# Six of the loads' input arrays laid out in DRAM as eight groups of sixteen rows

## Chip, core and metric

The kernel runs on one core of a Trainium2 chip. The metric is device time in microseconds of one execution. A difference of 2% is about 10 us here.

## What is computed

Two batches, 12 heads, 448 tokens, head width 64. First an attention whose scores are mixed across heads before the softmax and whose weights are mixed across heads after it; its output, as rows of 768 channels, goes through a mixer block and a gated block. Everything is float32; some weights arrive as float64 and are turned into pairs of rounded parts on the chip.

```
scores = scale * q @ k^T;  scores = einsum('bhij,hg->bgij', scores, w_pre)
attn = softmax(scores);    attn = einsum('bhij,hg->bgij', attn, w_post);  x = attn @ v
u = x + token mixing (relu(x^T w_tok1) w_tok2)^T;  x = u + relu(u w_ch1) w_ch2
h = gelu(x w_in); u, v = halves of h; v = layernorm(v) * g
out = x + (u * (w_sg v + b_sg)) w_out
```

## The kernel before

The order of all work is written out by hand; each engine runs its instructions in that order and waits on semaphores. The attention fills about the first 200 us and the three later blocks the rest.

**Chunks.** The queries of a batch are cut into four chunks of 120, 120, 120 and 88 (`CH`), so there are eight chunks. For one chunk, `qk` (matmuls of line 328) makes the scores of two heads at a time and a copy (line 333) puts them into a tile S, with 128 query slots on the partitions and 12 heads by 448 keys along each row.

**Steps.** To mix across heads, heads have to lie on partitions. So a chunk is cut into steps of 20 queries, 46 steps in all. For each step `b_dma` (line 360) issues two transfers, SBUF to SBUF, from S into a tile P of a ring of six: each reads ten partitions of S and writes 120 partitions of P, 12 heads for each query. `b_pre` (line 368) multiplies P by the mixing weights, the vector engine takes the row maximum (373), the scalar engine exponentiates (381), GpSimd makes the normalising weights (388 to 394), `b_post` (line 415) multiplies by the second mixing and transposes back in 64 small matmuls, and a copy (425) puts the result into AT. When a chunk's steps are done, `av` (lines 450 and 459) multiplies AT by v.

**The loop.** At index i the loop issues, if they are due, one `qk` of the next chunk, `b_pre` of step i+2, `b_post` of step i and then the transfers of step i+5 (`LD` = 5, `LP` = 2). A tile of the P ring is free again three steps later, so the P transfers can be three steps ahead of their matmul and no further. All DMAs but one are issued by SyncE (SP) in program order: the P transfers and the loads of q, k, v and weights share that queue.

**The loads.** q of one chunk comes in two loads (`load_q`, line 308), k of one batch in six (`load_k`, 315), v of one batch in three (`load_v`, 304). The list `loads` says at which index i each is issued: index -4 and -3 the third chunk's q, 1 and 3 the first batch's second and third v, 4 to 6 the fourth and fifth chunks' q and the first token weight (`w_dma`, line 99), 9 to 14 the second batch's k, and so on to 29. Four pieces of token weights (`w_tok1`, `w_tok2`) are loaded during the attention. The first three pieces of the channel weights are loaded by

```
        if 0 < i + LD - NB <= RB:
            w_dma()
```

with NB = 46 and RB = 3, thus at i = 42, 43 and 44. Every one of these loads writes 128 partitions from a DRAM array whose first axis has 128 rows.

**Layouts on the host.** `layouts` transposes the inputs before the launch; the arrays that it returns are the kernel's DRAM tensors.

Of the kernel before, what the change touches and what calls it, by code (L numbers as in the profile page):

```python
# [19 lines left out]
LD, LP = 5, 2  # L20
NP_BUFS = 2 * (LD - LP + 1)

WB, RB, SQ = 3, 3, 5
# [4 lines left out]


@with_exitstack  # L30
def tile_kernel(ctx, tc, q, k, v, w_pre, w_post, w_tok1, w_tok2, w_ch1, w_ch2,
                w_u, w_v, g_ln, w_sg, b_sg, w_out, out):
    nc = tc.nc
    B, D, H, S = 2, 64, 12, 448
    P = 128
# [1 line left out]
    C = H * D  # L37
    NCC = C // P
    T = B * S
    TOK = w_tok1.shape[2]  # L40
    NF = w_ch1.shape[1]
    DH = w_v.shape[2]
    ND = DH // P
# [2 lines left out]
    CH = [(0, 120), (120, 120), (240, 120), (360, 88)]  # L46
# [167 lines left out]
    def piece(src, pr, a, n, scale=None, dst=None):  # L214
        pieces.append([src, pr, a, n, scale, dst])
        return len(pieces) - 1
# [5 lines left out]
    NS = 4  # L222
    def tok_dst(n, pr, a, w):
        return lambda: [shared[:pr, 2 * n + j, :a * w].rearrange("p (a n) -> p a n", a=a) for j in range(2)]

    p_t1 = [piece(w_tok1[:, i:i + 2], P, 2, TOK, dst=tok_dst(i // 2, P, 2, TOK)) for i in range(0, NS, 2)]
    p_t2 = [piece(w_tok2[:, i:i + 1], P, 1, S, dst=tok_dst(NS // 2 + i, P, 1, S)) for i in range(TOK // P)]
    wvt = {}

    def wv_dst(cc):  # L230
# [68 lines left out]
    QG = 3  # L299
    NQ = NP // QG  # L300

    def load_v(b, g):
        t = vn[b, g] = ap_.tile([P, 14 * D], F32, tag=f"vn{g}", name=f"vn{b}_{g}")
        nc.sync.dma_start(out=t, in_=v[b, :, g])

    def load_q(b, c, g, eng=nc.sync):
        t = qn[b, c, g] = qp.tile([P, QG, P], F32, tag=f"qn{g}", name=f"qn{b}_{c}_{g}", bufs=2)
        eng.dma_start(out=t, in_=q[b, :, c, g * QG:(g + 1) * QG])

    KG = [(i, 1) for i in range(NP)]  # L310

    def load_k(b, g):
        i, n = KG[g]
        x = qp.tile([P, n, S], F32, tag=f"kn{g}", name=f"kn{b}_{g}")
        nc.sync.dma_start(out=x, in_=k[b, :, i:i + n])
        for j in range(n):
            KX[b, i + j] = x[:, j]

    def qk(x, i, pool=psM, copies=(nc.scalar.copy,)):

        b, c = chunks[x]
        if i == 0:
            SS[b, c] = qp.tile([P, SWC], F32, tag="S3", name=f"S{b}_{c}") if x % 3 == 1 else big(f"S{b}_{c}", F32)
        nm = f"qk{b}_{c}_{i}"
        ps = pair(nm, pool)
        for cols in HALVES:
            for j, rows in enumerate(HALVES):
                nc.tensor.matmul(ps[cols, j, :S], lhsT=qn[b, c, i // QG][rows, i % QG, cols], rhs=KX[b, i][rows],  # L328
                                 start=True, stop=True)
        n = 2 // len(copies)  # L330
        for j, copy in enumerate(copies):
            o = (2 * i + j * n) * S
            copy(SS[b, c][:, o:o + n * S].rearrange("p (j s) -> p j s", j=n), ps[:, j * n:(j + 1) * n, :S])  # L333
# [10 lines left out]
    NB = len(steps)  # L344
# [161 lines left out]
    for g in range(NQ):  # L506
        load_q(0, 1, g)
    load_const()
    load_v(0, 0)


# [14 lines left out]
    for x in range(NCH):  # L526
        if x < 2:
            at = [-LD - 1 + x] * NP
            for i in range(NP):
                n = x * NP + i  # L530
# [45 lines left out]
    for i in range(-LD, NB):  # L576
        for fn, a in extra.get(i, []):
            fn(*a)
        ahead = 0 <= i + LP < NB
        due = list(scores.get(i, []))  # L580
        if due:
            qk(*due.pop(0))
        if ahead:
            b_pre(i + LP)
        next_turn(i, 0)
        if ahead:
            b_max(i + LP)
        if 0 <= i + 1 < NB:
            b_norm(i + 1)
        for d in due:  # L590
            qk(*d)
        if i >= 0:
            b_post(i)
        if ahead:
            b_exp(i + LP)
        if i >= 0:
            b_turn(i, nc.scalar.copy if i - END in AT_ACT else nc.vector.tensor_copy)
            next_av(i)
        next_turn(i, 1)
        if i + LD < NB:  # L600
            b_dma(i + LD)
        for fn, a in loads.get(i, []):
            fn(*a)
        if 0 < i + LD - NB <= RB:
            w_dma()
        if i >= 8 and wstate["conv"] <= p_t2[-1]:
            pump(1)
        if i + LD == first[chunks[-1]] - 1:
            XR = [big(f"x{nm}0") for nm in "hl"]
            X[0] = [t[:, :XW] for t in XR]  # L610
            RX[0] = [t[:, XW + 16:XW + 16 + TOK // P * C].rearrange("p (t c) -> p t c", c=C) for t in XR]
        if i + LD == NB:
            qctx.close()
            wctx = ctx.enter_context(ExitStack())
            wpool = wctx.enter_context(tc.tile_pool(name="wp", bufs=1, side="right", reuse_waits="tile"))
            wstate["open"] = True
# [43 lines left out]
    with ExitStack() as mctx:  # L660
        mp = mctx.enter_context(tc.tile_pool(name="tok", bufs=1, reuse_waits="tile"))
        RR = {}
        def tok1(b, turns=()):
# [3 lines left out]
            got, pss = [], []  # L667
            for tt in range(TOK // P):
                ts = slice(tt * P, (tt + 1) * P)
# [12 lines left out]
            rest = [x[:, (NS - 1) * C:XW] for x in (xh, xl)]  # L682
            for tt in range(TOK // P):
                ts = slice(tt * P, (tt + 1) * P)
# [10 lines left out]
        def tok2(b):  # L695
# [3 lines left out]
            for cc in range(NCC):  # L699
                cs = slice(cc * P, (cc + 1) * P)  # L700
                ps = bank(f"t2ps{b}_{cc}")
                mm3(ps[:, :S], [((rh[:, tt, cs], rl[:, tt, cs]), t2[tt]) for tt in range(TOK // P)])
                U[cc, b] = later(add_split(cc, b, ps[:, :S], uh, ul))
# [211 lines left out]
def layouts(q, k, v, w_pre, w_post, moe_w_tok1, moe_w_tok2, moe_w_ch1, moe_w_ch2,  # L915
            moe2_w_in, moe2_g_ln, moe2_w_sg, moe2_b_sg, moe2_w_out):

    import numpy as np

    def bits(a):  # L920

        return a.view(np.uint64) if a.dtype == np.float64 else a

    def rows(a, p):

        return bits(a).reshape(-1, p, a.shape[1]).transpose(1, 0, 2)

    def blocks(a):

        n = a.shape[0] // 128 * 128  # L930
        return rows(np.concatenate([a, a[n:]]), 128)

    def cols(a, p):

        return bits(a).reshape(a.shape[0] // p, p, -1, p).transpose(1, 2, 0, 3)

    def diagonal(w):
        h = w.shape[0]
        t = np.zeros((2, 64, h, 5), w.dtype)
        for i in range(5):  # L940
            t[:, h * i:h * (i + 1), :, i] = w
        return t

    def spread(a):

        n = a.shape[-1]
        full, rest = n // 10, n % 10 // 2
        t = np.zeros((*a.shape[:-1], 128), a.dtype)
        rows = t[..., :120].reshape(*a.shape[:-1], 10, 12)
        rows[..., :full] = a[..., :10 * full].reshape(*a.shape[:-1], 10, full)  # L950
        if rest:
            rows[..., :rest, full:full + 2] = a[..., 10 * full:].reshape(*a.shape[:-1], rest, 2)
        t[..., :120] = rows.reshape(*a.shape[:-1], 120)
        return t

    def tokens(w):

        t = np.concatenate([w.T, w.T])
        return t.reshape(-1, 128, t.shape[1]).transpose(1, 0, 2)

    B, H, S, D = q.shape
    qt = q.reshape(B, H // 2, 2, S, D).transpose(0, 2, 4, 1, 3).reshape(B, 2 * D, H // 2, S)
    qt = np.stack([spread(qt[..., s:s + 120]) for s in range(0, S, 120)], 2)
    whole = S // 128 * 128
    vs = v.reshape(B, H // 4, 2, 2, S, D)
    vt = vs[..., :whole, :].reshape(B, H // 4, 4, S // 128, 128, D).transpose(0, 4, 1, 2, 3, 5)
    vr = v.reshape(B, 2, H // 4, 2, S, D)[..., whole:, :].transpose(0, 1, 4, 2, 3, 5).reshape(B, 128, H // 4, 2 * D)
    vt = np.concatenate([vt.reshape(B, 128, H // 4, -1), vr], -1)
    wp = diagonal(w_pre).transpose(0, 1, 3, 2).reshape(2, 64, 60)
    wp = np.pad(wp, ((0, 0), (0, 0), (0, 4)))  # L970
    wp[0] = np.roll(wp[0], 4, 0)
    wq = diagonal(w_post).reshape(128, 60)
    half = moe2_w_in.shape[1] // 2
    arrays = {
        'q': qt,
        'k': k.reshape(B, H // 2, 2, S, D).transpose(0, 2, 4, 1, 3).reshape(B, 2 * D, H // 2, S),
        'v': vt,
        'w_pre': wp.reshape(128, 64),
        'w_post': wq,
        'w_tok1': blocks(moe_w_tok1),  # L980
        'w_tok2': rows(moe_w_tok2, 128),
        'w_ch1': cols(moe_w_ch1, 128),
        'w_ch2': cols(moe_w_ch2, 128),
        'w_u': cols(np.ascontiguousarray(moe2_w_in[:, :half]), 128),
        'w_v': rows(np.ascontiguousarray(moe2_w_in[:, half:]), 128),
        'g_ln': moe2_g_ln.reshape(-1, 128).T,
        'w_sg': tokens(moe2_w_sg),
        'b_sg': moe2_b_sg.reshape(1, S),
        'w_out': cols(moe2_w_out, 128),
    }  # L990
    return {n: np.ascontiguousarray(a) for n, a in arrays.items()}
# [34 lines left out]
```

## Time and profile before

| | us |
|---|---|
| median of 3 runs | 508.65 |
| lowest and highest | 505.95 and 512.27 |
| the profiled execution's own time | 511.61 |
| its span, first to last instruction | 509.8 |

The span holds 14006 instructions. TensorE (PE) is busy for 95% of it, VectorE for 67%, ScalarE for 46%, GpSimd for 41%. The 16 DMA engines move 63.84 MB. Times below are in us from the span's start; "issue" as a releaser means that the engine waited for nothing that the profile shows, and SPq is SP's queue of DMA instructions.

### The profile page before, as it was taken

How to read it: one execution, taken by the hardware profiler on the slowest of the kernel's cores; microseconds unless marked ns; L12 is line 12 of the kernel's file. 1: busy time of each engine (PE TensorE's matmuls, PEld its weight loads, DVE VectorE, ACT ScalarE, POOL GpSimd, SP SyncE). 2: the span in 40 equal slices, each digit the busy share in tenths (PEclk: the TensorE clock that was granted, in tenths of full speed). 3: DMA queues.
4: the chain of work that ended last, by engine and by line, in shares of the span. 5: the costliest groups of instructions: out<-in, count | busy, mean ns of one | idle time of the engine just before them, and what ended most of it. 6: DMA issues, size and time to landing. Idle time of an engine off the chain costs nothing.

```text
span 509.8 us, 14006 instructions
## 1 busy us (share of the span) xinstructions
PE 485.2 (95%) x6010; PEld 411.8 (81%) x6010; DVE 342.6 (67%) x452; ACT 236.5 (46%) x457; POOL 208.7 (41%) x292
## 2 busy tenths in 40 slices
PE   9987999989799889999999999999999999999997
PEld 5455677756577569999999999999999998888896
DVE  4574566657365645963657687789887964897882
ACT  3675576576466434462434443333332345454320
POOL 2355256365355420284123322444554434258400
PEclk9999999999899999999999999999999999999999
DMA  6788364455523500310234343353432323103122
GB/s 225 231 227 232 139 219 154 153 200 179 171 112 139 205 4 2 125 63 27 98 103 145 125 143 105 123 165 101 149 123 88 119 73 124 32 0 123 68 85 109
DMA packets 26306, 63.84 MB, mean 125 GB/s; under 512 B 2900, under 2 KB 19844, under 8 KB 26244
## 3 DMA queue, kind: packets, MB, share of 16 engines
q1 hardware_dynamic: 26100, 62.75, 37.0%
q8 instruction: 47, 0.77, 0.6%
q10 hardware_dynamic: 144, 0.20, 0.1%
q14 instruction: 15, 0.12, 0.1%
HBM read 40.83 MB, written 2.75 MB: 85 GB/s over the span
## 4 chain that ended last, share of the span: by engine, by line
PE 89%; issue 4%; ACT 2%; DVE 2%; DMA 1%; POOL 1%; SPq 0%; POOLq 0%; ACTq 0%
PE qk L328 8%; PE post L415 8%; PE av L450 6%; PE c1ps L632 6%; PE c2ps L632 6%; PE pre L368 6%; PE c2ps L634 6%; PE c1ps L634 6%; PE c2ps L633 6%; PE c1ps L633 6%; PE ups L633 2%; PE ups L632 2%; PE ups L634 2%; PE vps L634 2%; PE vps L633 2%
## 5 line engine op out<-in xcount | busy, mean ns | idle before, releaser
L156 POOL TENSOR_TENSOR wl<-cv,wh 128x768 fp32r<-128x768 f32 x28 | 52.6, 1878 | 132.0 <-ACT wh L153 100.6
L415 PEld LDWEIGHTS post<-wt,E 60*64 60x64 f32 x2880 | 54.3, 138 | 31.8 <-issue 23.6
L381 ACT ACTIVATE E<-pre,nm 128x448 f32<-128x448 f32 x90 | 56.3, 632 | 37.3 <-DVE nm L373 33.4
L415 PE MATMUL post<-wt,E 60*64 60x60 f32 (+1 forms) x2880 | 56.3, 221 | 10.5 <-issue 8.3
L373 DVE TENSOR_REDUCE nm<-pre 128x2 f32<-128x896 f32 (+1 forms) x46 | 49.1, 1068 | 24.0 <-PE pre L368 22.2
L135 DVE SCALAR_TENSOR_TENSOR cv<-raw,cv 128x768 uint32<-128x768 uint32 (+2 forms) x44 | 53.1, 1207 | 1.2
L328 PE MATMUL qk<-kn,qn 64*64 64x448 f32 x384 | 50.0, 565 | 3.2 <-issue 1.9
L632 PE MATMUL c1ps<-uh,wh 128*128 128x448 f32 x144 | 52.3, 363 | 0.0
L632 PE MATMUL c2ps<-r1h,wh 128*128 128x448 f32 x144 | 52.3, 363 | 0.0
L368 PE MATMUL pre<-P,wp 64*64 64x448 f32 (+1 forms) x360 | 50.7, 547 | 1.7 <-ACT E L381 1.1
L634 PE MATMUL c2ps<-r1h,wl 128*128 128x448 f32 x144 | 52.2, 362 | 0.0
L634 PE MATMUL c1ps<-uh,wl 128*128 128x448 f32 x144 | 52.2, 362 | 0.0
L633 PE MATMUL c1ps<-ul,wh 128*128 128x448 f32 x144 | 51.8, 360 | 0.0
L633 PE MATMUL c2ps<-r1l,wh 128*128 128x448 f32 x144 | 51.8, 360 | 0.0
L425 DVE COPY AT<-post 128x840 f32<-128x840 f32 (+1 forms) x42 | 44.0, 1047 | 9.7 <-PE post L415 9.6
L113 ACT ACTIVATE cv<-raw 128x768 f32<-128x768 f32 (+2 forms) x44 | 36.1, 821 | 26.9 <-POOL wl L156 19.9
L388 POOL TENSOR_SCALAR rc<-sm 128x2 f32<-128x2 f32 (+1 forms) x46 | 10.5, 229 | 90.2 <-ACT E L381 89.7
L333 ACT COPY S<-qk 128x896 f32<-128x896 f32 x42 | 38.0, 905 | 17.4 <-PE qk L328 15.4
L137 DVE SCALAR_TENSOR_TENSOR cv<-raw,cv 128x768 uint32<-128x768 uint32 (+2 forms) x44 | 40.3, 915 | 1.0
L153 ACT CAST wh<-cv 128x768 fp32r<-128x768 f32 x28 | 23.4, 835 | 34.8 <-DVE cv L137 33.9
L655 DVE SCALAR_TENSOR_TENSOR r1l<-c1ps,r1h 128x448 fp32r<-128x448 f32 x24 | 15.0, 624 | 30.6 <-ACT r1h L653 30.6
L450 PE MATMUL av<-AT,vn 128*64 128x120 f32 (+1 forms) x576 | 32.5, 266 | 2.0 <-issue 1.9
(148 smaller groups left out, 1035.3 us busy)
## 6 DMA issues: line engine op xcount, KB each, us to landing
P<-S SPq DMA_DIRECT2D x88, 210.0 KB
raw<-in_w_ch_dram SPq DMA_DIRECT2D x24, 768.0 KB
raw<-in_w_v_dram SPq DMA_DIRECT2D x6, 512.0 KB
raw<-in_w_u_dram SPq DMA_DIRECT2D x4, 768.0 KB
raw<-in_w_out_dram SPq DMA_DIRECT2D x6, 512.0 KB
qn<-in_q_dram SPq DMA_DIRECT2D x15, 192.0 KB
kn<-in_k_dram SPq DMA_DIRECT2D x12, 224.0 KB
vn<-in_v_dram SPq DMA_DIRECT2D x6, 448.0 KB
```

Source lines behind the costliest of these rows:

```text
L135: nc.vector.scalar_tensor_tensor(fi, lo, 29, fi, op0=ALU.logical_shift_right, op1=ALU.bitwise_or)
L156: nc.gpsimd.tensor_tensor(dst[1], f, f32(dst[0]), op=ALU.subtract)
L328: nc.tensor.matmul(ps[cols, j, :S], lhsT=qn[b, c, i // QG][rows, i % QG, cols], rhs=KX[b, i][rows], start=True, stop=True)
L368: nc.tensor.matmul(ps[cols, e, :S], lhsT=wp[rs], rhs=ring[(2 * i + r) % NP_BUFS][rs], start=True, stop=True)
L373: nc.vector.tensor_reduce(out=st[i]["nm"][:, :ne], in_=st[i]["pre"][:, :ne, :S], axis=AX.X, op=ALU.max, negate=True)
L381: nc.scalar.activation(t, st[i]["pre"][:, e, :S], AF.Exp, bias=st[i]["nm"][:, e:e + 1], scale=1.0, accum_out=sm[:, e:e + 1])
L415: nc.tensor.matmul(ps[cols, r, o:o + w.stop - w.start], lhsT=E[rs, t * 64:(t + 1) * 64], rhs=wt[rs, w], start=True, stop=True)
L425: copy(dst, src)
L450: nc.tensor.matmul(into(hp, x, j), lhsT=vn[b, hp // 2][:, ((hp % 2 * 2 + j) * NH + s) * D:][:, :D], rhs=at[:, s * H + 2 * hp + j, :cols], ...
L632: nc.tensor.matmul(ps, lhsT=lh, rhs=rh, start=(start and i == 0), stop=False)
L633: nc.tensor.matmul(ps, lhsT=lh, rhs=rl, start=False, stop=False)
L634: nc.tensor.matmul(ps, lhsT=ll, rhs=rh, start=False, stop=(stop and i == n - 1))
```

## The change

The arrays `q` (from the third chunk on), `k` (second batch), `v` (both), `w_tok1` and `w_tok2` are laid out as 8 groups of 16 rows with one row of zeros behind each group, and the loads read `[:, :16]` of them. The first two chunks of q and the first batch of k become arrays of their own, `q0` and `k0`, with 128 plain rows. The destinations in SBUF and the indices at which the loads are issued are as they were. The condition on `w_dma` becomes `NB - RB <= i`, thus i = 43, 44 and 45.

```diff
-    p_t1 = [piece(w_tok1[:, i:i + 2], P, 2, TOK, dst=tok_dst(i // 2, P, 2, TOK)) for i in range(0, NS, 2)]
-    p_t2 = [piece(w_tok2[:, i:i + 1], P, 1, S, dst=tok_dst(NS // 2 + i, P, 1, S)) for i in range(TOK // P)]
+    p_t1 = [piece(w_tok1[:, :16, i:i + 2], P, 2, TOK, dst=tok_dst(i // 2, P, 2, TOK)) for i in range(0, NS, 2)]
+    p_t2 = [piece(w_tok2[:, :16, i:i + 1], P, 1, S, dst=tok_dst(NS // 2 + i, P, 1, S)) for i in range(TOK // P)]
...
-        nc.sync.dma_start(out=t, in_=v[b, :, g])
+        nc.sync.dma_start(out=t, in_=v[b, :, :16, g])
...
-        eng.dma_start(out=t, in_=q[b, :, c, g * QG:(g + 1) * QG])
+        n = b * len(CH) + c
+        src = q0[:, n] if n < 2 else q[:, :16, n - 2]
+        eng.dma_start(out=t, in_=src[..., g * QG:(g + 1) * QG, :])
...
-        nc.sync.dma_start(out=x, in_=k[b, :, i:i + n])
+        nc.sync.dma_start(out=x, in_=k[:, :16, i:i + n] if b else k0[:, i:i + n])
...
-        if 0 < i + LD - NB <= RB:
+        if NB - RB <= i:
             w_dma()
...
+    def apart(a, d=0):
+
+        a = a.reshape(*a.shape[:d], 8, 16, *a.shape[d + 1:])
+        t = np.zeros((*a.shape[:d + 1], 17, *a.shape[d + 2:]), a.dtype)
+        t[(slice(None),) * (d + 1) + (slice(16),)] = a
+        return t
...
-        'q': qt,
-        'k': k.reshape(B, H // 2, 2, S, D).transpose(0, 2, 4, 1, 3).reshape(B, 2 * D, H // 2, S),
-        'v': vt,
+        'q0': qt[:, :2],
+        'q': apart(qt[:, 2:]),
+        'k0': kt[0],
+        'k': apart(kt[1]),
+        'v': apart(vt, 1),
...
-        'w_tok1': blocks(moe_w_tok1),
-        'w_tok2': rows(moe_w_tok2, 128),
+        'w_tok1': apart(blocks(moe_w_tok1)),
+        'w_tok2': apart(rows(moe_w_tok2, 128)),
```

## Rows read from the trace of the kernel before

**Rows 1.** The page, busy time and share of the span of TensorE.

```profile
PE 485.2 (95%) x6010; PEld 411.8 (81%) x6010; DVE 342.6 (67%) x452; ACT 236.5 (46%) x457; POOL 208.7 (41%) x292
```

**Rows 2.** Waits of TensorE: engine, line, releaser: total us, times, longest.

```profile
PE post L415 <- issue: 8.3, 8, 3.1
...
PE qk L328 <- issue: 1.9, 1, 1.9
...
PE pre L368 <- DMA P<-S: 0.5, 2, 0.3
```

**Rows 3.** Timeline of TensorE: start, us, instruction, count [idle before, releaser].

```profile
32.13 0.91 PE L415 MATMUL post<-wt,E 60*64 60x60 f32 x49 [1.13 <-issue]
...
48.86 1.16 PE L415 MATMUL post<-wt,E 60*64 60x30 f32 x33 [3.09 <-issue]
...
136.24 0.59 PE L328 MATMUL qk<-kn,qn 64*64 64x448 f32 x2 [1.94 <-issue]
...
186.91 0.43 PE L415 MATMUL post<-wt,E 60*64 60x60 f32 x16 [1.39 <-issue]
```

**Rows 4.** The page, DMA queues: packets, MB, share of 16 engines.

```profile
q8 instruction: 47, 0.77, 0.6%
```

**Rows 5.** Stretches: busy us and count per engine, clock, DMA share, GB/s.

```profile
123.10:127.70 4.60, 3.78 (x136) 2.67 (x129) 3.61 (x5) 2.95 (x7) 3.05 (x8) 1.00 0.79 245
127.70:134.00 6.30, 5.41 (x130) 4.06 (x127) 2.50 (x4) 3.16 (x8) 2.67 (x5) 1.00 0.74 210
...
185.00:188.00 3.00, 1.43 (x55) 1.02 (x47) 0.92 (x1) 1.02 (x3) 1.12 (x3) 1.00 0.00 0
```

**Rows 6.** The same view, stretches after two long pauses of TensorE.

```profile
48.80:52.20 3.40, 3.34 (x52) 2.41 (x56) 1.06 (x1) 0.47 (x1) 2.73 (x4) 0.51 0.81 237
...
137.50:141.00 3.50, 3.50 (x70) 2.80 (x69) 2.10 (x2) 1.99 (x5) 0.05 (x1) 0.51 0.32 123
```

**Rows 7.** The same view: channel weights alone, and mostly P transfers.

```profile
170.00:174.00 4.00, 3.99 (x160) 3.57 (x162) 4.00 (x5) 1.98 (x7) 1.58 (x6) 1.00 1.00 399
20.00:23.00 3.00, 3.00 (x107) 2.05 (x103) 2.17 (x3) 1.63 (x7) 1.66 (x5) 1.00 0.65 218
```

**Rows 8.** The page, DMA issues: count and KB of each.

```profile
P<-S SPq DMA_DIRECT2D x88, 210.0 KB
...
qn<-in_q_dram SPq DMA_DIRECT2D x15, 192.0 KB
...
vn<-in_v_dram SPq DMA_DIRECT2D x6, 448.0 KB
...
raw<-in_w_tok_dram SPq DMA_DIRECT2D x2, 512.0 KB
```

**Rows 9.** The chain that ended last, in order of time: start, us, what.

```profile
15.43 3.77 DMA P<-S
...
19.34 0.52 PE pre L368
```

**Rows 10.** Timeline of SP's queue, 13 to 58 us.

```profile
14.08 0.44 SPq L308 DMA_DIRECT2D qn<-in_q_dram  x1
...
16.29 0.46 SPq L308 DMA_DIRECT2D qn<-in_q_dram  x1
16.80 7.03 SPq L360 DMA_DIRECT2D P<-S  x8
23.88 0.67 SPq L304 DMA_DIRECT2D vn<-in_v_dram  x1
...
28.12 0.50 SPq L304 DMA_DIRECT2D vn<-in_v_dram  x1
```

**Rows 11.** Waits of SP's queue between 28 and 42 us.

```profile
SPq L360 <- DMA P<-S: 2.6, 4, 0.7
```

**Rows 12.** Timeline of SP's queue, 157 to 205 us.

```profile
156.45 11.43 SPq L360 DMA_DIRECT2D P<-S  x8
167.93 37.10 SPq L99 DMA_DIRECT2D raw<-in_w_ch_dram  x4
```

More of the change, by code (lines that the diff above doesn't have):

```diff
@@ L30, in tile_kernel @@
 @with_exitstack
-def tile_kernel(ctx, tc, q, k, v, w_pre, w_post, w_tok1, w_tok2, w_ch1, w_ch2,
+def tile_kernel(ctx, tc, q0, q, k0, k, v, w_pre, w_post, w_tok1, w_tok2, w_ch1, w_ch2,
                 w_u, w_v, g_ln, w_sg, b_sg, w_out, out):
@@ L39, in tile_kernel @@
     T = B * S
-    TOK = w_tok1.shape[2]
+    TOK = w_tok1.shape[3]
     NF = w_ch1.shape[1]
@@ L963, in layouts @@
     qt = np.stack([spread(qt[..., s:s + 120]) for s in range(0, S, 120)], 2)
+    qt = qt.transpose(1, 0, 2, 3, 4).reshape(2 * D, -1, H // 2, 128)
+    kt = k.reshape(B, H // 2, 2, S, D).transpose(0, 2, 4, 1, 3).reshape(B, 2 * D, H // 2, S)
     whole = S // 128 * 128
```

## The prediction, made before the changed kernel was run

> **What bounds the kernel now.** I read the busy times first. TensorE works for 485.2 us [rows 1], so the whole span has only about 25 us in which it does nothing; an edit of loads can win something there or lengthen it, and nothing else. The next view is the list of TensorE's waits [rows 2]. Almost nothing of it is a wait for data: the P transfers appear with 0.5 us. The two largest entries are "issue", 8.3 us before the second mixing and 1.9 us before the scores. So I looked for those pauses in the timeline [rows 3]: 3.09 us at 45.7, 1.94 us at 134.3, shorter ones between, each in the middle of a run of equal matmuls whose operands were there.
>
> Two rows say what they are. The queue named "instruction" carries 47 packets of 0.77 MB [rows 4], 16 KB each, and TensorE has 6010 + 6010 instructions: 256 for each packet. Between one pause and the next TensorE runs 136 + 129 = 265 instructions, then 130 + 127 = 257 [rows 5]. So TensorE pauses where a block of its code ends and the next has not come; that code comes through the same DMA engines as the loads. The pause does not need traffic: at 185.5 it is 1.39 us [rows 3] in a stretch where the DMA engines move nothing [rows 5]. The two longest are behind heavy traffic, and after each the clock is granted at about half, 1.2 instead of 2.4 GHz, for some 3.4 us [rows 6].
>
> The DMA engines come next. When three channel-weight loads are alone, all 16 engines are full and move 399 GB/s, 25 GB/s each. When nearly only P transfers are in flight the share stands at 0.65 and 218 GB/s [rows 7]: about ten engines are full and six idle, which fits the ten partitions that a P transfer reads. In that stretch a P of 210 KB [rows 8] needs about 0.99 us (215 KB at 218 GB/s) and SP issues one each 0.88 us (eight in 7.03 us [rows 10]), so a backlog builds on those ten engines. It shows twice: the chain waits 3.77 us for one P at the start [rows 9], and between 28 and 42 us SP itself stops four times until a P has landed [rows 11].
>
> By a rule of the Trainium skill (DMA: Bandwidth & Descriptors, "Why a DMA increments its semaphore by 16 and not by 1") a transfer takes the largest number of engines up to 16 that divides the slowest dimension of both sides, and the lowest-numbered ones. That makes ten for P, which the share of 0.65 bears out, and eight for the new loads, all eight among P's ten. That speaks against the change; which engines carry a load no row shows. My sum needs only that 10 + 8 is more than 16.
>
> **The change part by part.**
>
> *Loads on eight engines.* Bytes stay. At 25 GB/s per engine a load of 192 KB of q takes 0.49 us on 16 engines and 0.98 on eight; v (448 KB) 1.15 and 2.30; a first token weight (512 KB) 1.31 and 2.62. So each engine that carries it works 0.49, 1.15 or 1.31 us longer, and the others not at all. With ten engines under P, at least two are shared, and a P has landed only when its slowest engine is done. So each P behind a load comes later by those 0.49 to 1.31 us wherever the backlog stands, and none comes earlier.
>
> *The start, where P is on the path.* In front of the P that the chain waits for (issued at 15.43, matmul at 19.34) stands the q load of 14.08, then the q load of 16.29, v at 23.88 and v at 28.12 [rows 9, 10]. Lower end: the first q alone, +0.5. Upper end: all four on the path, 0.49 + 0.49 + 1.15 + 1.15 = +3.3. After 19.34 nearly every P came before its matmul, so there is some margin that no row measures. I take both q loads and half of one v: **+1.6 us**. What is late then is `b_pre`, and behind it in TensorE's order the same index's `b_post`.
>
> *Code blocks.* The load's packets and the code share engines. A block that sits on one of the eight waits up to one load's extra time longer, on one of the other eight up to its present share less; no row shows which engine carries a block. Gain end: the nine pauses of rows 2 on these two lines, 8.3 + 1.9 = 10.2 us, less the 1.39 that comes without traffic, so 8.8, and both clock dips, 2 x 1.7 (half of 3.4), together -12.2. Loss end: eight pauses longer by one v, 8 x 1.15 = 9.2, and one more dip of 1.7, +10.9. The bytes per core stay the same and half of the blocks gain, so the ends nearly cancel; but a block that comes early gives nothing beyond its pause, while a late one is paid in full. I take **+1.0 us**. The Trainium skill (Runtime: NRT & Kernel Launch, "Instruction fetch mechanics") has code refilled in blocks of 256 instructions, as rows 4 and 5 bear out, and calls the cost of a block's end mostly hidden, which the 3.09 us of rows 3 contradict. By that rule this term would be nothing and the sum 1.0 us less.
>
> *Later P transfers, k, q, v and token weights.* After about 60 us SP mostly stops for a free place in the ring, no longer for a landing, so a P that lands one load later (0.5 to 1.3 us) is covered by the up to three steps between issue and matmul. TensorE's row for P (0.5 us in all) says that this cover holds; if it went, each step would pay up to 1.2. q, k and v are issued several steps before use, token weights tens of us before theirs: nothing. SP's instruction for such a load, 0.46 us now, may grow toward P's 0.88; SP waits elsewhere, so nothing.
>
> *The index of `w_dma`.* Nothing else is issued on SP in these steps: P's last issue is followed at 167.93 by the channel loads [rows 12]. The order in SP's queue is the same, so nothing; GpSimd and ScalarE issue none of them. The loads' first use is after 200 us.
>
> Sum: 1.6 + 1.0 = +2.6 us on the profiled execution's 511.61, which gives 514.2. That execution lies 2.96 above the median of 508.65; against the median the forecast is **511.3 us**, which is no change by what can be told here (2%, 10 us).
>
> **Rivals.**
>
> *Code comes free (faster).* If the blocks behind the two long pauses sit on the unloaded engines, these pauses shrink to the quiet 1.39: 1.70 + 0.55 = 2.25 us, and both dips go, 3.4. With the start's +1.6 that is -4.0, 504.6; if all pauses go, -12.2 + 1.6 = -10.6, 498.0. For it: the long pauses lie in the heaviest traffic [rows 5, 6]. Against it: the bytes remain, and 1.39 us come with no traffic at all. Chance 0.22.
>
> *P becomes the bound (slower).* Between 14 and 47 us five q, two v and a token weight are loaded: 5 x 0.49 + 2 x 1.15 + 1.31 = 6.1 us more on each shared engine. If the backlog on P's engines is the limit throughout, which it is once P lands after the matmul before it in TensorE's order is done, all of it is paid, with a further clock dip of 1.7 and the 1.0 of the code: +8.8, 517.4, and up to 522 if the second batch's start does likewise. For it: SP already stops for landings [rows 11]. Against it: TensorE hardly waits for P after the start [rows 2]. Chance 0.18.
>
> *The loads do not take eight engines*, or it does not matter where they lie: 508.65. Against it: P's ten rows do limit P [rows 7]. Chance 0.10.
>
> **How the numbers follow.** The forecast, a few us more or less around 511, has 0.50. The first rival spreads from 498 to 507, the second from 514 to 522, and medians of three runs here scatter by some 3 us. Below 503 lies about 0.08, above 519 about 0.09, so the range is 503 to 519. Faster by over 2% (under 498.5) needs the first rival at its end: 0.04. Slower by over 2% (over 518.8) is half of the second rival and a little of the forecast: 0.11. Within 2%: 0.85.
>
> **What would show it.** Right: in a stretch with only such a load in flight the DMA share stands near one half and the landing takes twice as long; the 3.77 us for P at the start grow by 0.5 or more and P appears among TensorE's waits between 15 and 36 us; the issue pauses at the ends of code blocks stay at about 10 us together, some longer, some shorter. The first rival shows as pauses at 45 and 134 us of about 1.4 us and no dip behind them. The second shows as several us of waits for P up to 55 us, with SP stopped by landings for longer than 2.6 us. The forecast is wrong if TensorE's issue waits change by over 5 us, or if P's waits exceed 4.

## The result and the profile after

The changed kernel takes 513.93 us (median of 14 runs, 509.94 to 518.14) against 509.19 for the kernel before (14 runs, 504.34 to 515.16). The ratio is 1.0106, 95% interval 1.0065 to 1.0147: about 5 us slower, clear of the scatter and within 2%. Runs marked slow, which lie some 1.5% above the fastest of their kernel, are in the medians and left out of the ratios, so that a ratio here can lie off the quotient of its medians; both executions profiled for this section are marked so.

That the loads take eight engines shows in the page's packet count. First the kernel before, then after:

```profile
DMA packets 26306, 63.84 MB, mean 125 GB/s; under 512 B 2900, under 2 KB 19844, under 8 KB 26244
```

```profile
DMA packets 26082, 63.84 MB, mean 124 GB/s; under 512 B 2676, under 2 KB 19620, under 8 KB 26020
```

The bytes are the same and 224 of the smallest packets are gone: 28 loads from five arrays were changed (12 of q, 6 of k, 6 of v, 4 token weights), which makes eight packets for each load, one for each engine that it no longer uses.

Busy time on the page after, against [rows 1]: TensorE works one us longer in a span that is 6.6 longer, so the rest is waiting.

```profile
PE 486.4 (94%) x6010; PEld 412.3 (80%) x6010; DVE 342.8 (66%) x452; ACT 236.3 (46%) x457; POOL 209.6 (41%) x292
```

TensorE's waits after (line numbers have moved by two; engine, line, releaser: us, times, longest), against [rows 2]:

```profile
PE post L417 <- issue: 8.8, 6, 3.2
PE av L452 <- ACT S L335: 4.7, 1, 4.7
PE pre L370 <- DMA P<-S: 2.0, 2, 1.5
PE qk L330 <- issue: 1.9, 1, 1.9
...
PE qk L330 <- DMA qn<-in_q_dram: 0.8, 1, 0.8
```

The issue pauses are much as they were, P has gone from 0.5 to 2.0, q is new, and a single wait of 4.7 us for a copy of the scores by ScalarE is new. The timeline of TensorE after, against [rows 3], places them:

```profile
19.73 1.40 PE L370 MATMUL pre<-P,wp 64*64 64x448 f32 x6 [1.48 <-DMA P<-S]
...
55.13 3.36 PE L452 MATMUL av<-AT,vn 128*64 128x120 f32 x36 [4.73 <-ACT S L335]
...
139.58 0.59 PE L330 MATMUL qk<-kn,qn 64*64 64x448 f32 x2 [1.95 <-issue]
147.49 0.78 PE L417 MATMUL post<-wt,E 60*64 60x60 f32 x29 [3.18 <-issue]
```

What held ScalarE is in the chain after, in order of time (start, us, what), against [rows 9]:

```profile
15.45 4.14 DMA P<-S
...
31.16 10.44 DMA P<-S
...
41.62 11.98 DMA raw<-in_w_tok_dram
...
53.62 0.02 ACT cv L113
...
54.19 0.90 ACT S L335
```

The first token weight, issued at 41.62, lands 11.98 us later. ScalarE's instruction for it stands ahead of the copy of the scores in ScalarE's order. The same instruction of line 113 in ScalarE's timeline, first before, then after:

```profile
47.79 0.66 ACT L113 ACTIVATE cv<-raw 128x512 f32<-128x512 f32 x1
```

```profile
53.62 0.66 ACT L113 ACTIVATE cv<-raw 128x512 f32<-128x512 f32 x1 [4.27 <-DMA raw<-in_w_tok_dram]
```

Before, the weight was there when ScalarE came to it; after, ScalarE stood for 4.27 us, the copy and then `av` behind it. What this costs can be read from the matmuls of `b_pre` on either side of it, the same two before and after:

```profile
44.33 0.99 PE L368 MATMUL pre<-P,wp 60*64 60x448 f32 x8
...
57.98 1.14 PE L368 MATMUL pre<-P,wp 64*64 64x448 f32 x8
```

```profile
45.79 0.96 PE L370 MATMUL pre<-P,wp 64*64 64x448 f32 x8
...
59.75 1.13 PE L370 MATMUL pre<-P,wp 64*64 64x448 f32 x8
```

From one to the other are 13.65 us before, with code pauses of 3.09 and 1.05, and 13.96 after, with the wait of 4.73. Against this execution of the kernel before the wait costs 0.3 us, because it stands where two pauses stood; how long those are in other executions comes below.

SP's queue too now stops for loads, where it stopped for P [rows 11]:

```profile
SPq L317 <- DMA raw<-in_w_tok_dram: 4.3, 1, 4.3
SPq L310 <- DMA vn<-in_v_dram: 3.4, 2, 2.3
```

One stretch shows such a load nearly by itself. From 10.0 to 11.5 us after, almost nothing but the first v load is in flight, on eight engines:

```profile
10.00:11.50 1.50, 1.50 (x24) 0.73 (x20) 1.21 (x3) 0.90 (x2) 0.00 (x0) 1.00 0.42 151
```

It moves 151 GB/s, where half of the 399 of [rows 7] would be 200. But its DMA share is 0.42 and not 0.50, so the eight engines were not full throughout: 151 / (0.42 x 16) is 22.5 GB/s for each while it is busy, against 25. In a second execution of the changed kernel the same stretch has 177 GB/s at a share of 0.45, 24.6 for each; in the first, 9 to 10 us has 135 at 0.50, 16.9 for each. So the 448 KB of v take somewhat longer than the 2.3 us of the prediction, and how much slower an engine is on such a load is open. Over the whole run it doesn't show: the page puts the packets of the data queue at 37.0% of 16 engines' 509.8 us before, which is 189 us, and after at 37.4% of 516.4 and 36.5% of 512.5, 193 and 187.

### The profile page after: what moved, and what is told of

Read it like the earlier page. It is cut to its first block, busy times and chain, and to the rows that moved or that the text cites. A ratio compares the mean times of both kernels' runs of the same rounds, so it can differ in the third digit from the quotient of the medians.

```text
span 516.4 us, 14006 instructions
## 1 busy us (share of the span) xinstructions
PE 486.4 (94%) x6010; PEld 412.3 (80%) x6010; DVE 342.8 (66%) x452; ACT 236.3 (46%) x457; POOL 209.6 (41%) x292
## 3 DMA queue, kind: packets, MB, share of 16 engines
q1 hardware_dynamic: 25876, 62.75, 37.4%
## 4 chain that ended last, share of the span: by engine, by line
PE 85%; DMA 5%; issue 4%; ACT 2%; DVE 1%; SPq 1%; POOL 1%; POOLq 0%; ACTq 0%
PE post L417 7%; PE av L452 6%; PE qk L330 6%; PE c1ps L634 6%; PE c2ps L634 6%; PE c2ps L636 6%; PE c1ps L636 6%; PE c2ps L635 6%; PE c1ps L635 6%; PE pre L370 5%; DMA P<-S 3%; DMA raw<-in_w_tok_dram 2%; PE ups L635 2%; PE ups L634 2%; PE ups L636 2%
## 5 line engine op out<-in xcount | busy, mean ns | idle before, releaser
L417 PEld LDWEIGHTS post<-wt,E 60*64 60x64 f32 x2880 | 53.0, 134 | 31.8 <-issue 23.4
L417 PE MATMUL post<-wt,E 60*64 60x60 f32 (+1 forms) x2880 | 54.7, 218 | 11.0 <-issue 8.8
L330 PE MATMUL qk<-kn,qn 64*64 64x448 f32 x384 | 48.4, 550 | 4.1 <-issue 1.9
L452 PE MATMUL av<-AT,vn 128*64 128x120 f32 (+1 forms) x576 | 35.2, 281 | 5.1 <-ACT S L335 4.7
L452 PEld LDWEIGHTS av<-AT,vn 128*64 128x64 f32 x576 | 31.6, 150 | 6.1 <-ACT S L335 4.8
```

Of the source, the lines that this page charges most:

```text
L417: nc.tensor.matmul(ps[cols, r, o:o + w.stop - w.start], lhsT=E[rs, t * 64:(t + 1) * 64], rhs=wt[rs, w], start=True, stop=True)
L452: nc.tensor.matmul(into(hp, x, j), lhsT=vn[b, hp // 2][:, ((hp % 2 * 2 + j) * NH + s) * D:][:, :D], rhs=at[:, s * H + 2 * hp + j, :cols], ...
```

## The experiments

Twelve runs were made, in four batches with five rounds each; ratios are against the kernel before on the same chip, with the 95% interval. An edit "plain" below means that the array goes back to 128 rows and the load to its old slice; the slices are left out of the cuts, and so is the old condition on `w_dma`, to which the runs with one or two kinds of array in groups go back.

### Which array costs

**q alone.** From the changed kernel:

```diff
-        'k': apart(kt[1]),
-        'v': apart(vt, 1),
+        'k': kt[1],
+        'v': vt,
...
-        'w_tok1': apart(blocks(moe_w_tok1)),
-        'w_tok2': apart(rows(moe_w_tok2, 128)),
+        'w_tok1': blocks(moe_w_tok1),
+        'w_tok2': rows(moe_w_tok2, 128),
```

> Of the change only q from the third chunk is in 8 groups; k, v and the token weights are read from 128 plain rows, w_dma at its old index. Theory A (separate prices: the q loads of the third chunk hold up P at the start, the first token weight holds up ScalarE, the second batch's v and token weight hold up code blocks): TensorE waits for P about 2 us between 14 and 24 us, no wait of ScalarE for the token weight, time +1.5 to +2.5 against the kernel before, about 511. Theory B (the layout with a gap, not the eight engines, makes loads slow): the same here, so this run does not tell A from B. Theory C (one backlog for all: each load adds its share of 6 us): about +2 of some 6.

Measured 1.0006 (0.9975 to 1.0037). The wait for P at the start is there in its timeline, and still the time is that of before; the +1.5 to +2.5 us fell.

```profile
19.67 1.39 PE L370 MATMUL pre<-P,wp 64*64 64x448 f32 x6 [1.64 <-DMA P<-S]
```

**Token weights alone** (q, k, v plain).

```diff
-        'q': apart(qt[:, 2:]),
+        'q': qt[:, 2:],
```

> Of the change only the two token weights' arrays are in 8 groups. Theory A: the start is as before; ScalarE's first conversion (L113) waits for the first token weight for 1 to 4 us, less than the 4.27 of the changed kernel as the queue in front of it is shorter, and TensorE pauses behind it; but the code pause of 3.09 us at 45.7 lies in the same place and overlaps it; time +1 to +4. Theory C: +1.3 (one load's extra time on the shared engines).

Measured 0.9969 (0.9923 to 1.0015). ScalarE waited 3.1 us for the weight, but the code pause lay over it, here 4.74 us. No loss is seen; the expected +1 to +4 fell.

**All but the token weights** (only they plain).

```diff
-        'w_tok1': apart(blocks(moe_w_tok1)),
+        'w_tok1': blocks(moe_w_tok1),
```

> The changed kernel with the token weights back on 128 plain rows. Theory A: no wait of ScalarE for the token weight (4.27 us in the changed kernel); the start stays 2 us late; time 2 to 5 us below the changed kernel, so about 510 to 511. If the wait for the token weight only hides another (P, or a code block, takes its place): within 1.5 us of the changed kernel.

Measured 1.0127 (1.0087 to 1.0167), no better than the whole change; the 2 to 5 us fell. Its waits of TensorE:

```profile
PE qk L330 <- DMA qn<-in_q_dram: 2.3, 1, 2.3
PE av L452 <- ACT S L335: 2.2, 1, 2.2
PE pre L370 <- DMA P<-S: 1.7, 1, 1.7
```

With the token weight on 16 engines q became the late one (2.3 in place of 0.8), and ScalarE still waited 1.7 us for the token weight, which stands in the queue behind the same backlog. The wait changed its name and stayed.

**v alone, k alone, all but v.** Each with one or more of the lines above, for example

```diff
-        'q': apart(qt[:, 2:]),
-        'k': apart(kt[1]),
+        'q': qt[:, 2:],
+        'k': kt[1],
```

> Of the change only v is in 8 groups. Theory D (v is the part that costs: the largest load at the busiest places; q alone and the token weights alone left the time where it was, and the change without the token weights kept all of its loss): +3 to +6 us against the kernel before, most of it in code pauses between 107 and 150 us. Theory E (no part alone costs; the loss comes only with q, k and v together, when the loads' extra times add up to a backlog that lasts): within 1.5 us of the kernel before.

> Of the change only the second batch's k is in 8 groups. Theory D: within 1.5 us of the kernel before. A rival of D, that k is the part (two k loads at 47 to 49 us reach the full queue and delay the second batch's scores): +2 to +5 us, with waits of TensorE for k or for the copies of the scores behind 60 us. Theory E: within 1.5 us.

> The changed kernel with v back on 128 plain rows. Theory D: 0 to +1.5 us against the kernel before, code pauses after 107 us as in the kernel before; the wait of ScalarE for the first token weight stays, 2 to 4 us. Theory E: +2 to +4 us, a loss in proportion to the loads that are left.

Measured, in this order: v alone 1.0060 (1.0019 to 1.0101), k alone 1.0074 (1.0032 to 1.0117), all but v 1.0035 (0.9991 to 1.0079). Neither theory D (v carries it) nor E (no part costs alone) holds: alone, v costs some 3 us and k nearly 4. How k does it isn't shown: with k alone TensorE has no wait for k, and its issue waits, 14.6 us together, are those of before (14.2).

**k and v together** (q and token weights plain).

```diff
-        'q': apart(qt[:, 2:]),
+        'q': qt[:, 2:],
```

> Of the change only k and v are in 8 groups; q and the token weights plain, w_dma as before. Theory F (the parts add): 0.74 + 0.60 = +1.3%, 5 to 8.5 us against the kernel before, as much as the whole change or a little more. Rival (they share one cost, for example the same code pauses, which only one of them can lengthen): +0.6 to +0.9%.

Measured 1.0052 (1.0000 to 1.0104), less than the 1.3% of a plain sum. So the parts' single values, each uncertain by some 0.4%, don't settle how the loss divides among the arrays.

### Eight engines, or the gaps

The same arrays in 16 groups of 8 rows and in 4 groups of 32, each group with a row of zeros behind it:

```diff
-        a = a.reshape(*a.shape[:d], 8, 16, *a.shape[d + 1:])
-        t = np.zeros((*a.shape[:d + 1], 17, *a.shape[d + 2:]), a.dtype)
-        t[(slice(None),) * (d + 1) + (slice(16),)] = a
+        a = a.reshape(*a.shape[:d], 16, 8, *a.shape[d + 1:])
+        t = np.zeros((*a.shape[:d + 1], 9, *a.shape[d + 2:]), a.dtype)
+        t[(slice(None),) * (d + 1) + (slice(8),)] = a
```

```diff
+        a = a.reshape(*a.shape[:d], 4, 32, *a.shape[d + 1:])
+        t = np.zeros((*a.shape[:d + 1], 33, *a.shape[d + 2:]), a.dtype)
+        t[(slice(None),) * (d + 1) + (slice(32),)] = a
```

> The changed kernel with the same arrays in 16 groups of 8 rows, one row of zeros behind each, so that the layout has gaps but a load can take 16 engines. Theory A (eight engines): as the kernel before within 1 us, no wait for the token weight, TensorE's wait for P 0.5 us, code pauses at 45 and 134 us again. Theory B (the gaps): as the changed kernel, +5 us.

> The changed kernel with the same arrays in 4 groups of 32 rows, one row of zeros behind each, so that a load can take four engines. Theory A (the number of engines): a load's extra time on its engines is three times that of eight (64 KB of q, k's 56 and v's 112 KB per engine more than on 16 are then 3/16 of the load in place of 1/16); the loss of 1.06% becomes about 3%, +12 to +20 us, with long waits of TensorE for P, for q and k, and of ScalarE for the token weight. Rival B (the gaps in the layout): as the kernel with 16 groups, 0 to +1%.

Measured 1.0046 (1.0001 to 1.0091) with 16 groups and 1.0632 (1.0567 to 1.0696) with four. With 16 groups the packet count is 26306, that of before, and with four 25970, that is 28 x 12 fewer: the loads take 16 and four engines. With the gaps kept, 16, 8 and 4 engines give +0.5, +1.1 and +6.3%. Four engines cost far more than the same gaps do with 16; the loss is twice what was expected (whose 64 KB of q is 48, 192 / 4; its 3/16 of a load stands).

The step from 16 to 8 isn't clear by the times alone: the intervals overlap, and the medians of all runs are 0.9% above the kernel before in both (512.85 against 508.37, and 513.93 against 509.19). What tells these two apart are the waits. With 16 groups TensorE's list has no wait for P, for q or behind the copy for `av`, and ScalarE waits 0.2 us for the first token weight. So these waits come from the number of engines; how much of the 1.06% does, and how much comes from the gaps, is open. That gaps cost something is hinted at by the first v load: between 8.5 and 10 us the kernel before moves 263 GB/s at a DMA share of 0.70, 23.5 for each busy engine, and the one with 16 groups 233 at 0.96, 15.2 (one execution each).

TensorE's waits with four groups:

```profile
PE qk L330 <- DMA qn<-in_q_dram: 9.9, 2, 6.2
PE pre L370 <- DMA P<-S: 7.8, 4, 2.4
PE av L452 <- ACT S L335: 5.0, 1, 5.0
PE qk L330 <- ACT S L335: 4.4, 2, 3.4
PE av L452 <- DMA vn<-in_v_dram: 2.5, 1, 2.5
PE qk L330 <- DMA kn<-in_k_dram: 1.4, 1, 1.4
...
PE post L417 <- issue: 0.3, 1, 0.3
```

Here the signs of the change stand enlarged: q, P, v, k and, through ScalarE, the token weights (14.0 us of ScalarE's waits), 31 us together. The pauses at the ends of code blocks, 8.3 before on that line, are 0.3; that the code has time to come while TensorE waits for data would explain it, and is not tested. TensorE also works longer, 494.8 us against 485.2 for the same 6010 matmuls, at a mean granted clock of 0.962 against 0.990. So waiting makes up 16.9 of the 26.5 us between these two spans, and slower matmuls 9.6.

### The index of w_dma, and the conversion

Only the new condition, with q0 and k0 as arrays of their own and every load plain:

```diff
-        if 0 < i + LD - NB <= RB:
+        if NB - RB <= i:
```

> Of the change only the new condition on w_dma (i = 43 to 45) and the splitting off of q0 and k0 as arrays of their own; every load from 128 plain rows. Theory F (the loss is the sum of the arrays' own parts: q +0.06%, k +0.74, v +0.60, token weights -0.31, together +1.09% against +1.06 measured for the whole): 0, within 1.5 us of the kernel before. Rival (the excess of 0.46% of the kernel with 16 groups comes from this rest of the change, not from its gaps): +1.5 to +3 us.

Measured 0.9968 (0.9922 to 1.0015): nothing, as predicted; the rival, which gave it the 0.46% of the 16 groups, falls.

The changed kernel with a later start of the conversion on ScalarE:

```diff
-        if i >= 8 and wstate["conv"] <= p_t2[-1]:
+        if i >= 12 and wstate["conv"] <= p_t2[-1]:
```

> The changed kernel with the conversion of the early token weights begun at index 12 of the loop in place of 8, so that ScalarE does not come to it before its load has landed. Theory: TensorE's 4.7 us behind the copy of the scores goes; if it is paid in full, the time falls by 3 to 5 us against the changed kernel; if it only stands in the place of a code pause (3.09 us at 45.7 in the kernel before), the pause comes back and the time falls by 0 to 2 us.

Measured 1.0171 (1.0116 to 1.0225) against the kernel before, no gain on the changed kernel's 1.0106. The trace shows the gain and its loss:

```profile
54.51 1.14 PE L370 MATMUL pre<-P,wp 64*64 64x448 f32 x8
...
64.94 0.55 PE L417 MATMUL post<-wt,E 60*64 60x60 f32 x24 [2.74 <-issue]
...
70.08 1.09 PE L370 MATMUL pre<-P,wp 60*64 60x448 f32 x8
```

The first line is the matmul that starts at 59.75 in the changed kernel and at 57.98 in the kernel before: without the wait, and with no long code pause in its place, TensorE is there 5.2 us earlier than in the changed kernel. By the last line, which the kernel before reaches at 68.22 and the changed kernel at 70.52, the lead is gone: a code pause of 2.74 us, and behind it a granted clock of 0.74 and 0.69 in the stretches 65 to 68 and 68 to 71. Later the collision came back elsewhere: ScalarE waited 3.2 us for the third token weight, and `av` 2.76 us behind it at 133. So in these traces the wait is paid in full where no pause of code stands over it, and the gain was lost to the next pause.

### What of a trace repeats

> The changed kernel once more, unchanged, for a second profiled execution. Theory G (the lateness of the loads is the kernel's own and repeats, the long code pauses and clock dips are chance of one execution, as the trace of the kernel with only w_dma changed has 0.35 us where the kernel before had 3.09): TensorE again waits 1 to 2.5 us for P before 24 us, ScalarE again 3 to 5 us for the first token weight and TensorE 3 to 5 us behind it; the code pauses above 2 us stand at other places or are missing. Rival (the two traces of before and after differ by what the change does, pause by pause): 3.18 us at 144 and 1.95 us at 137 again, none above 0.6 between 30 and 60 us. Time against the kernel before +0.6 to +1.5% in both.

Measured 1.0144 (1.0046 to 1.0241). TensorE's waits in this second execution of the changed kernel, then a line of its ScalarE's timeline and one of its TensorE's:

```profile
PE post L417 <- issue: 7.5, 5, 3.4
PE av L452 <- issue: 2.9, 2, 2.5
PE pre L370 <- DMA P<-S: 1.9, 1, 1.9
```

```profile
52.70 0.66 ACT L113 ACTIVATE cv<-raw 128x512 f32<-128x512 f32 x1 [3.31 <-DMA raw<-in_w_tok_dram]
```

```profile
50.62 0.70 PE L417 MATMUL post<-wt,E 60*64 60x30 f32 x33 [3.37 <-issue]
```

P's 1.9 us and ScalarE's 3.31 us for the token weight repeat. The code pauses don't: 3.37 us now stand at 47, where the first execution had none, and lie over the token weight's wait, so TensorE doesn't wait for ScalarE; nothing stands at 144, where the first had 3.18. In the run with only w_dma changed, whose loads are those of before, the same line has

```profile
PE post L417 <- issue: 4.2, 6, 1.4
```

against the 8.3 and the 3.1 of [rows 2]. It reaches the matmul of 57.98 at 54.45, with 0.35 and 0.38 us where the kernel before paused for 3.09 and 1.05. The mean granted clock differs too (span and clock): first that run, then the changed kernel's second execution.

```profile
core 0: 502.0 us, clock 0.999
```

```profile
core 0: 512.5 us, clock 0.983
```

What the clock lacks is worth, by an estimate that takes TensorE as always busy, 0.001 x 502 = 0.5 us in the one and 0.017 x 512.5 = 8.7 in the other. Part of this goes with the change: in this round the mean granted clock is 0.987 over the six runs of the changed kernel and 0.994 over the eleven of the kernel before, and over all rounds 0.990 in the fourteen runs of the result and 0.993 in the 92 of the kernel before. By the same estimate the lower clock carries some 1.6 to 3.5 us of the loss. Where the 6.6 us between the two first traces lie is thus chance in good part, while the 5 us of the ratio stand on fourteen runs of each. Theory G holds but for the 3 to 5 us of TensorE behind the token weight; its rival falls.

## Why the prediction was right, and where not

- **The sum and the sign.** Forecast 511.3, +2.6 us, range 503 to 519, and within 2%; measured 513.93 and +1.06%, about +5.4 us. Inside the range, the right side of zero, half the size. The range holds both no change and twice the loss, so the number alone says little for the mechanism.
- **Ten engines under P, at least two shared.** That loads on fewer engines make P late is shown by the dose: with 16 groups TensorE has no wait for P in its list (0.5 and 0.8 us in two executions with plain loads), with 8 it waits 2.0 and 1.9 us, with 4 7.8, and the time is +0.5, +1.1 and +6.3%. Which engines carry a load is still not shown.
- **Bytes stay, time per engine doubles.** The doubling is borne out, the rate only in part: a busy engine moved 16.9 to 24.6 GB/s in three stretches of the v load on eight, against the 25 taken from [rows 7]; over the whole run the engine time didn't grow beyond its scatter (193 and 187 us against 189). The share that was to stand near one half is 0.42 and 0.45.
- **The start, +1.6 us.** TensorE's waits for P went from 0.5 to 2.0 and 1.9 in two executions: the mechanism was right. The P of [rows 9] landed after 4.14 us in place of 3.77, +0.37, where 0.5 or more was named as the sign; of the four loads only the first q stands in front of it. The term's size fits further on: the matmul of `b_pre` that starts at 29.71 before starts 2.07 us later after, though the run with only w_dma changed is itself 1.15 late there. At 36.59 only 0.46 of this is left, as the code pause of 1.13 us before 32.13 [rows 3] is missing after. That q alone, whose wait for P is 2.0, left the time unchanged agrees: the wait was not paid in full at the end.
- **Code blocks, +1.0 us.** Not settled. Issue waits of TensorE summed over the lines listed were 14.2 us before and 12.9 and 12.0 after, but 9.1 in the run with only w_dma changed: this scatter is larger than the term, and the 5 us named as a sign of being wrong pass without the change. The step treated the 3.09 us as the kernel's own; it is one execution's. The clock stood in it as one dip of 1.7 us at its loss end; by the estimate above it is 1.6 to 3.5 us.
- **Token weights: nothing.** This step failed. It had them needed tens of us after their issue; SP issued the first at 38.3 and ScalarE converted it at 47.79, nine us later, and in front of a copy of the scores. After the change ScalarE waited 4.27 and 3.31 us there. The wait costs 0.3 us against an execution with long code pauses in that place and about 5 against one without, and that the token weights alone, or all but them, did not move the time accordingly fits: it is one of several waits that hide one another.
- **Index of `w_dma`: nothing.** Right, 0.9968 (0.9922 to 1.0015).
- **First rival, code comes free.** With four groups the code pauses did go, to 0.3 us on their main line, and the kernel was 6.3% slower: here they went together with long waits for data. Its gain did not come.
- **Second rival, P becomes the bound.** Not at eight engines. At four, P has 7.8 us and the loads themselves more. Its price of 8.8 us was too high at eight; that it added loads whose lateness lies over the same pauses is likely, and not tested by itself.

Left open: how the 5 us divide among q, k, v and the token weights; which engine carries a block of code; whether the gaps by themselves cost up to 0.9%, and so how much of the 1.06% is due to the number of engines. No version beat the kernel before.

## What to carry to other kernels

A load on half of the engines is not slow for itself alone: what comes behind it can wait too, as P did here, and the first stage to wait was the one whose backlog already stood. Before costing a late load at nothing, look in every engine's own order for its first reader and for what stands behind that reader. Where pauses move from one execution to the next, compare medians of many runs for the size and use a trace only for what repeats in two of them.

## What the runs showed of the hardware that was not expected

- On eight engines one v load nearly alone moved 151 and 177 GB/s in two executions (10.0 to 11.5 us), 22.5 and 24.6 for each busy engine, and 135 in an earlier stretch, 16.9 for each, against 25 with 16 engines and three loads.
- Executions of one program differ by up to 12 us here (499.81 to 511.75 in the run with only w_dma changed), with mean granted clocks from 0.987 to 0.999. At the end of the same block of code TensorE paused 0.35 us in one execution, 3.09 and 4.74 in others whose code is the same there.
- Where waits for data were long, nearly all pauses at code block ends were missing (8.3 to 0.3 us on one line), and the clock was lower: 0.962 against 0.990 with four groups, so that the same matmuls took 9.6 us longer.
